# A fixed program order for attention's output projection, with its LayerNorm finished on ScalarE

## The chip, the cores and the metric

One core of a Trainium2 chip runs the whole kernel as one program. The metric is the device time of one execution in microseconds. Five engines work side by side, each through its own queue in order: TensorE (matmuls and transposes), VectorE, ScalarE, GpSimd, and SyncE, which here only issues DMA transfers.

## The reference

A pre-LayerNorm transformer block: sliding-window attention, then a gMLP whose gate mixes the 2048 positions by a matrix. S is 2048, D is 640, 32 heads of 20, window 256, hidden width 864.

```
def _A_ref(x, wqkv, wo):                      # attention
    q, k, v = split_heads(x @ wqkv)
    scores = einsum("bhqd,bhkd->bhqk", q, k) * Dh ** -0.5
    mask = (i - j >= 0) & (i - j < 256)
    p = softmax(where(mask, scores, -1e9))
    return merge_heads(einsum("bhqk,bhkd->bhqd", p, v)) @ wo

def _B_ref(x, w_in, w_sp, b_sp, w_out):       # gMLP
    z = gelu(x @ w_in)
    z1, z2 = z[..., :Fh], layernorm(z[..., Fh:])
    g = einsum("ts,bsf->btf", w_sp, z2) + b_sp[None, :, None]
    return (z1 * g) @ w_out

h = x + _A_ref(layernorm(x), A_wqkv, A_wo)
h2 = h + _B_ref(layernorm(h), B_w_in, B_w_sp, B_b_sp, B_w_out)
```

## The kernel before

The 2048 positions are 16 tiles of 128 rows. The stages follow each other: LayerNorm, q, k, v; attention by heads in groups of four; the output projection with the residual and the second LayerNorm; the gMLP's input projection (`z_pair`, `z2_pair`); the gate (`first_gate`, `second_gate`), and the output. Every matrix product is made of three products of split operands: a high part (a rounded copy) and a remainder (the operand minus the high part), so each product of two operands is high by high, high by remainder, remainder by high.

**The stage that the diff touches** is the loop over `i` in `range(NT)` near the end of `block_kernel`. For tile i it does this:

- `load_o` brings two tiles of attention output, stored in `o_d` by heads, into a buffer `m` and, by the function it returns, the reciprocals of the softmax sums from `r_d`. There are two such buffers, so the load for tiles 6 and 7 takes the place of tiles 2 and 3.
- `norm_o` multiplies the two on VectorE. `split_o` makes the high part (a copy on ScalarE, line 156) and the remainder (a subtraction on GpSimd, line 157).
- `proj_o` is the projection: 30 matmuls of 128x320 in `gemm` (line 91) into an accumulator `wo_ps`. There are two of those (`acc_tile`). Tiles 0 and 1 are projected earlier, while attention ends (`pre_ps`).
- The residual `xh` is added on VectorE (line 1160), the sum is stored in `h_d` by a DMA that ScalarE issues, and `layernorm` takes statistics on VectorE (lines 75 and 76), computes the reciprocal deviation on GpSimd (lines 77 and 78), and normalizes on VectorE (line 81).
- `turn_h(i - 2)` transposes the normalized tile on TensorE (line 806, into `ht_ps`), copies it out on ScalarE (`ho`), and stores it in `hn_d`, from which the gMLP's input projection reads it.
- Between these, `w1` (the generator `win1_prep`) prepares weights of the gMLP (`wraw` to `zl`), and `run(i - NT)` the first operands of the gMLP (`fx` to `aw`).

Before this loop stands attention's end. Its softmax sums are part of `o_d`. `inverse_sums` reads each quarter of them back from there (`inv`), takes the reciprocal on VectorE (line 348) and stores it in `r_d`; the last quarter can only be read when the last attention outputs (`ot`) have been written.

What sets the order: attention is inside `tc.manual_schedule` for TensorE, VectorE and ScalarE, so their instructions keep the order of the program. This ends with `ms.close()` ahead of the loop. From there the scheduler of the framework orders all engines by its own simulated times, and may put instructions of later iterations, or of later stages, ahead of earlier ones. GpSimd and SyncE are ordered by it in the loop in any case.

Of the kernel before, what the change touches and what calls it, by code (L numbers as in the profile page):

```python
# [7 lines left out]
F32 = mybir.dt.float32  # L8
F32R = mybir.dt.float32r
BF16 = mybir.dt.bfloat16  # L10
AF = mybir.ActivationFunctionType
OP = mybir.AluOpType
# [3 lines left out]
P = 128  # L16
S = 2048
D = 640
H = 32
DH = 20  # L20
NT = S // P
# [13 lines left out]
def block_kernel(ctx, tc, x, wqk, wv, wo, w_in, wsp, bsp, w_out, out):  # L35
    nc = tc.nc
    ms = ctx.enter_context(ExitStack())
# [3 lines left out]
    def pool(stack, name, **kw):  # L41
        return stack.enter_context(tc.tile_pool(name=name, bufs=1, reuse_waits="tile", **kw))

    const = pool(ctx, "const")
# [20 lines left out]

    def stat_tiles(i):
        st = const.tile([P, 2, 6], F32, tag="st", bufs=2, name=f"st{i}")
        mv = const.tile([P, 4], F32, tag="mv", bufs=3, name=f"mv{i}")
        return st, mv

    def layernorm(dst, src, n, key, between=None):
        st, mv = stat_tiles(key)
        hn = n // 2
        for j in range(2):
            nc.vector.bn_stats(out=st[:, j, :], in_=src[:, j * hn:(j + 1) * hn])
        nc.vector.bn_aggr(out=mv[:, 0:2], in_=st)
        nc.gpsimd.tensor_scalar(out=mv[:, 2:3], in0=mv[:, 1:2], scalar1=EPS, scalar2=None, op0=OP.add)
        nc.gpsimd.tensor_tensor(out=mv[:, 3:4], in0=mv[:, 2:3], in1=half, op=OP.pow)
        if between is not None:
            between()  # L80
        nc.vector.tensor_scalar(out=dst, in0=src, scalar1=mv[:, 0:1], scalar2=mv[:, 3:4],
                                op0=OP.subtract, op1=OP.mult)

    def gemm(ps, n, lhs, rhs, ks):

        lh, ll = lhs
        rh, rl = rhs
        for k in range(ks):
            for a, b in ((lh, rh), (lh, rl), (ll, rh)):
                for j in range(2):  # L90
                    nc.tensor.matmul(ps[:, j, :n], a(k), b(k, j),
                                     start=(k == 0 and a is lh and b is rh),
                                     stop=(k == ks - 1 and a is ll))
# [22 lines left out]
    def t1(lo, *shape):  # L116
        return view(mem["t1"], lo, *shape)

    def m1(lo, *shape):
        return view(mem["m1"], lo, *shape)  # L120
# [6 lines left out]
    def load_x2(i):  # L127
        hs[i] = mem["xh"][i % 5]
        nc.sync.dma_start(hs[i], x[i * P:(i + 1) * P, :])

    def load_o(j):

        t = slice(2 * j * P, (2 * j + 2) * P)
        ot, rs = m1(j % 2 * 2 * D, KD, 2 * P), m1(6 * D + j % 2 * 2 * P, 2 * P)
        for k in range(KD):
            nc.sync.dma_start(ot[:, k], o_d[:, 4 * k:4 * k + 4, t])
        for i in range(2):
            ots[2 * j + i] = (ot[:, :, i * P:(i + 1) * P], rs[:, i * P:(i + 1) * P])

        def load_rs():  # L140
            base = r_d[:, t]
            nc.sync.dma_start(rs, bass.AP(tensor=base.tensor, offset=base.offset, ap=[[S, H], [0, 4], [1, 2 * P]]))

        return load_rs

    def norm_o(i, eng):
        ot, rs = ots[i]
        eng.tensor_tensor(out=ot, in0=ot, in1=rs[:, None, :].to_broadcast([P, KD, P]), op=OP.mult)

    def split_o(i, eng):  # L150
        ot, _ = ots[i]
        osp = mem["osp2"] if i % 3 == 2 else t1((2 * KD + i % 3 * 2) * D, 2, KD, P)
        if eng is nc.vector:
            eng.tensor_copy(out=osp[:, 0], in_=ot)
        else:
            nc.scalar.activation(osp[:, 0], ot, AF.Copy)
        eng.tensor_tensor(out=osp[:, 1], in0=ot, in1=osp[:, 0].bitcast(F32), op=OP.subtract)
        ots[i] = osp

    def proj_o(i, ps):  # L160
        osp = ots.pop(i)
        wo_s = t1(0, 2, KD, D)
        gemm(ps, HD, [lambda k, p=p: osp[:, p, k, :] for p in range(2)],
             [lambda k, j, p=p: wo_s[:, p, k, j * HD:(j + 1) * HD] for p in range(2)], KD)
        return ps
# [35 lines left out]
    with ExitStack() as ab:  # L201
# [220 lines left out]
        if True:  # L422
# [8 lines left out]
            def ln1(i, between=None):  # L431
                xn = tmp.tile([P, D], F32, tag="tb", bufs=2, name=f"xn{i}")
                layernorm(xn, xts.pop(i), D, f"a{i}", between)
                xns[i] = xn
# [97 lines left out]
            c = halves[0]  # L532
# [73 lines left out]
        early, pre_ps = None, []  # L606
# [47 lines left out]
                pass  # L654


    ms.close()
    psK = ctx.enter_context(ExitStack())

    def acc_tile(name):  # L660
        return pools["c"].tile([P, 2, 512], F32, tag="acc", bufs=2, name=name)
# [6 lines left out]
    def bank(tag, name):  # L668
        if "d" not in pools:
            psK.close()  # L670
            pools["d"] = pool(ctx, "psD", space=PSUM)
        return pools["d"].tile([P, 512], F32, tag=tag, bufs=4, name=name)
# [56 lines left out]
    def hn(i):  # L729
        return m1((4 + i % 2) * D, D)  # L730
# [5 lines left out]
    def win1_prep(raw):  # L736
        seven, last = win1
        src = w_in[:, :FH].rearrange("k (h c) -> k h c", h=2)
        for k in range(2):
            for b in range(2):  # L740
                r = (k + 2 * b) * P
                nc.sync.dma_start(raw[:, b], src[r:r + P])
            yield
            yield
            for f in right_blocks(lambda: [s[k] for s in seven], *(raw[:, b, h] for b in range(2) for h in range(2)),
                                  eng=nc.gpsimd):
                f()
                yield
        nc.sync.dma_start(raw[:, 0], src[4 * P:])
        yield  # L750
        yield
        for j in range(2):
            split(*two(last[j]), raw[:, 0, j])
        yield
# [42 lines left out]
    def turn_h(i):  # L797
        ht = mem["ho"][i % 3]
        if i < NT - 2:
            ps = aux_tile(f"ht_ps{i}").rearrange("p a b -> p (a b)")  # L800
            parts = [(0, KD, ps)]
        else:
            parts = [(0, 4, bank("b", f"ht_a{i}")), (4, KD, bank("b", f"ht_b{i}"))]
        for k0, k1, ps in parts:
            for k in range(k0, k1):
                nc.tensor.transpose(ps[:, (k - k0) * P:(k - k0 + 1) * P], hn(i)[:, k * P:(k + 1) * P], ident)
            copy(ht[:, k0 * P:k1 * P], ps[:, :(k1 - k0) * P])
        nc.sync.dma_start(hn_d[i], ht)
# [90 lines left out]
    def z2_pair(q, i, j, k):  # L899
# [35 lines left out]
        def stat(t, h):  # L935
            if h == 0:
                stats[t] = stat_tiles(f"z{q}_{t}")
            st, mv = stats[t]
            nc.vector.bn_stats(out=st[:, h, :], in_=blocks[2 * t + h])
            if h:  # L940
                nc.vector.bn_aggr(out=mv[:, 0:2], in_=st)
                nc.gpsimd.tensor_scalar(out=mv[:, 2:3], in0=mv[:, 1:2], scalar1=EPS, scalar2=None, op0=OP.add)
                nc.gpsimd.tensor_tensor(out=mv[:, 3:4], in0=mv[:, 2:3], in1=half, op=OP.pow)
# [193 lines left out]
    def run(n):  # L1137
        for f in later.pop(n, []):
            f()
        if 0 <= n < len(steps):  # L1140
            steps[n][0]()
            steps[n][1]()

    w1 = win1_prep(mem["wraw"])
    for i in range(NT):
        if 1 < i + 1 < NT:
            split_o(i + 1, nc.gpsimd)
        if i % 2 == 0 and i + 4 < NT:
            load_o(i // 2 + 2)()
        if i + 2 < NT:  # L1150
            norm_o(i + 2, nc.vector)
        for n in (2, 3, 4) if i == 0 else (i + 4,) if i + 4 < NT else ():
            load_x2(n)
        run(i - NT)
        ps = pre_ps[i] if i < 2 else proj_o(i, acc_tile(f"wo_ps{i}"))
        if i > 1:
            turn_h(i - 2)
        xt = hs.pop(i)
        h3 = xt.rearrange("p (a b) -> p a b", a=2)
        nc.vector.tensor_tensor(out=h3, in0=ps[:, :, :HD], in1=h3, op=OP.add)  # L1160
        nc.scalar.dma_start(h_d[i], xt)
        layernorm(hn(i), xt, D, f"c{i}")
        next(w1, None)
        if i % 2:
            next(w1, None)
    for _ in w1:
        pass
    w2p = None
    for n in range(len(steps)):
        run(n)  # L1170
# [10 lines left out]
    n = NT - 2  # L1181
# [3 lines left out]
    ps = [bank("b", f"out_l{j}") for j in range(2)]  # L1185
# [30 lines left out]
```

## Time and profile before

| | us |
|---|---|
| median of 3 runs | 1148.1 |
| lowest, highest run | 1143.98, 1149.98 |
| span of the profiled execution | 1144.7 |
| TensorE busy in that span | 1096.0 (96%) |
| VectorE busy | 746.7 (65%) |
| ScalarE busy | 535.8 (47%) |
| GpSimd busy | 405.5 (35%) |

The profile gives the span as the profiled execution's own time, and no other; it lies within the three runs. In the profile's lines PE is TensorE, PEld its weight loads, DVE VectorE, ACT ScalarE, POOL GpSimd, SPq and ACTq the DMA queues of SyncE and ScalarE. A timeline row gives start, duration, engine, line, operation, output and inputs, and in square brackets how long the engine stood before it and what ended that. The projection loop lies between about 476 and 565 us of the span.

### The profile page before, as it was taken

The numbers are of one execution on the slowest core, as the hardware profiler recorded it, in microseconds if no ns is written. First come the engines' busy times: TensorE is split into PE (matmuls) and PEld (weight loads), VectorE is DVE, ScalarE is ACT, GpSimd is POOL, SyncE is SP. The second block draws the span as 40 slices with busy tenths as digits, with TensorE's granted clock in tenths as the row PEclk, the third lists the DMA queues.
The fourth block names the chain that finished last, engine by engine and source line by source line (L and its number), as shares of the span: only waits on it lengthen the run. The fifth ranks groups of instructions, "written<-read, shape, count | busy, mean of one in ns | idle before, by whom it ended". The sixth has DMA issues, their size and how long they took to land. (4 is left out here: it accounts for less than half of the span.)

```text
span 1144.7 us, 27633 instructions
## 1 busy us (share of the span) xinstructions
PE 1096.0 (96%) x10652; PEld 983.2 (86%) x10652; DVE 746.7 (65%) x1963; ACT 535.8 (47%) x1165; POOL 405.5 (35%) x553
## 2 busy tenths in 40 slices
PE   6999999999999999888999998999999899999998
PEld 6998887668788786788999997999999799999998
DVE  5541113789999996599677588455558974556543
ACT  3333433259999899344266554333334421222210
POOL 4124444547777678376220263000126410000000
PEclk9999999999999999899999998999999999999999
DMA  6212565656666635588455411323331463344322
GB/s 196 70 36 94 169 217 175 211 185 196 203 203 215 200 119 181 177 273 280 181 178 179 164 59 38 102 102 124 123 112 53 162 214 117 122 145 136 107 71 80
DMA packets 83844, 170.84 MB, mean 149 GB/s; under 512 B 11008, under 2 KB 47360, under 8 KB 79872
## 3 DMA queue, kind: packets, MB, share of 16 engines
q1 hardware_dynamic: 81408, 163.83, 44.3%
q10 hardware_dynamic: 2304, 5.24, 1.2%
q8 instruction: 83, 1.36, 0.5%
q14 instruction: 49, 0.40, 0.1%
HBM read 112.37 MB, written 56.23 MB: 147 GB/s over the span
## 5 line engine op out<-in xcount | busy, mean ns | idle before, releaser
L369 ACT ACTIVATE pt<-bank 128x384 f32<-128x384 f32 (+2 forms) x512 | 201.6, 496 | 13.9 <-PE bank L366 10.2
L1013 PE MATMUL g<-zl,aw 128*128 128x432 f32 x768 | 174.4, 362 | 7.3 <-ACT zl L681 4.9
L681 ACT ACTIVATE aw<-fx 128x512 fp32r<-128x512 f32 (+2 forms) x160 | 92.7, 595 | 187.6 <-PE g L1013 120.7
L312 DVE CUSTOM_DVE_ANT_0 junk<-bank,strip 128x288 bf16<-128x288 f32 x392 | 157.3, 454 | 6.6 <-PE bank L300 3.7
L1013 PEld LDWEIGHTS g<-zl,aw 128*128 128x128 f32 x768 | 144.8, 189 | 16.3 <-ACT zl L681 5.9
L1013 PE MATMUL g<-ze,aw 128*128 128x432 f32 x576 | 138.1, 368 | 6.0 <-DVE row L675 3.8
L675 DVE TENSOR_TENSOR aw<-fx,aw 128x512 fp32r<-128x512 f32 (+2 forms) x152 | 108.6, 723 | 37.2 <-ACT aw L681 36.7
L394 PE MATMUL pv<-pt,v_sb 128*32 128x192 f32 (+3 forms) x1984 | 126.8, 322 | 4.2 <-POOL pt L371 2.4
L1013 PEld LDWEIGHTS g<-ze,aw 128*128 128x128 f32 x576 | 109.2, 192 | 13.8 <-issue 3.2
L366 PE MATMUL bank<-slot 123*32 123x288 bf16 (+6 forms) x1536 | 107.0, 282 | 2.1 <-ACT pt L369 1.1
L371 POOL TENSOR_SCALAR_AFFINE_SELECT pt<-pt 128x512 f32<-128x512 f32 x128 | 84.0, 657 | 48.7 <-ACT pt L369 47.9
L1052 PE MATMUL out_ps<-wout,y_sp 128*128 128x320 f32 (+1 forms) x630 | 96.2, 310 | 0.4 <-ACT y_sp L124 0.4
L1052 PEld LDWEIGHTS out_ps<-wout,y_sp 128*128 128x128 f32 (+1 forms) x630 | 94.1, 188 | 1.3 <-ACT y_sp L124 0.7
L917 PE MATMUL zb<-win,aw 128*128 128x432 f32 x480 | 95.2, 359 | 0.0
L917 PEld LDWEIGHTS zb<-win,aw 128*128 128x128 f32 x480 | 90.0, 188 | 4.5
L300 PE MATMUL bank<-slot 120*32 120x288 bf16 (+2 forms) x1264 | 89.6, 286 | 0.0
L498 DVE TENSOR_TENSOR rest<-qk,sg 128x512 f32<-128x512 f32 x40 | 27.7, 691 | 85.7 <-ACT sg L496 85.7
L675 DVE TENSOR_TENSOR row<-g,row 128x432 f32<-128x432 f32 x80 | 48.0, 603 | 38.0 <-PE g L1013 32.5
L374 POOL TENSOR_SCALAR_AFFINE_SELECT pt<-pt 128x512 f32<-128x512 f32 x112 | 72.3, 645 | 0.0
L501 POOL TENSOR_TENSOR sg<-rest,sg 128x512 bf16<-128x512 f32 x40 | 46.6, 1164 | 72.1 <-ACT sg L500 68.9
L394 PEld LDWEIGHTS pv<-pt,v_sb 128*32 128x32 f32 x1984 | 59.4, 110 | 10.5 <-POOL pt L371 4.5
L366 PEld LDWEIGHTS <-slot 123*32 123x32 bf16 x1536 | 52.6, 97 | 17.2 <-issue 6.0
(189 smaller groups left out, 2172.7 us busy)
## 6 DMA issues: line engine op xcount, KB each, us to landing
fx<-wsp_in SPq DMA_DIRECT2D x32, 512.0 KB
slot<-qk_d SPq DMA_DIRECT2D x72, 200.0 KB
qk_d<-sg SPq DMA_DIRECT2D x32, 384.0 KB
slot<-qk_d SPq DMA_DIRECT2D x72, 160.0 KB
fx<-hn_d SPq DMA_DIRECT2D x32, 320.0 KB
o_d<-ot SPq DMA_DIRECT2D x64, 128.0 KB
z_d<-row SPq DMA_DIRECT2D x16, 432.0 KB
g_d<-row SPq DMA_DIRECT2D x16, 432.0 KB
```

Source lines behind the costliest of these rows:

```text
L300: nc.tensor.matmul(ps[32 * j:32 * j + 32, :n], part(st, half, 120, 0, hh, q0, 32), part(st, half, 120, 1, hh, lo + skip * j, n), start=Tru ...
L312: nc.vector.tensor_tensor_reduce(out=junk[:, :n], in0=ps[:, :n], in1=keep, scale=1.0, scalar=NEG, op0=OP.add, op1=OP.max, accum_out=m_cols ...
L366: nc.tensor.matmul(ps[32 * i:32 * i + 32, b:e], part(st, half, 123, 1, hh, k0, 32), part(st, half, 123, 0, hh, kb * P + b, e - b), start=T ...
L369: nc.scalar.activation(pt[:, hh, :n], ps[:, :n], AF.Exp, scale=SCALE)
L371: nc.gpsimd.affine_select(out=pt[:, :, :P], in_=pt[:, :, :P], pattern=[[0, 4], [1, P]], base=0, channel_multiplier=-1, compare_op=OP.is_ge ...
L374: nc.gpsimd.affine_select(out=pt[:, :, 256:], in_=pt[:, :, 256:], pattern=[[0, 4], [-1, P]], base=-1, channel_multiplier=1, compare_op=OP. ...
L394: nc.tensor.matmul(ps[32 * hh:32 * hh + 32, a - 512 * c:b - 512 * c], v_sb[:, kb, v0:v0 + 32], pt[:, hh, a - kb * P:b - kb * P], start=fir ...
L675: (eng or nc.vector).tensor_tensor(out=out, in0=a, in1=b, op=op)
L681: nc.scalar.activation(out, a, AF.Copy)
L917: nc.tensor.matmul(b[0][:, :HF], a[t][:, x, kk], win2[0][:, y, kk, h * HF:(h + 1) * HF], start=kk + x + y == 0, stop=kk == KD - 1 and x == 1)
L1013: nc.tensor.matmul(ps, w[m][:, x, k], zc[k][m][:, y], start=start and k + x + y == 0, stop=stop and k == 3 and x == 1, skip_group_check=True)
L1052: nc.tensor.matmul(ps[j][:, :HD], src[:w, a, k, :], e1["wout"][:w, b, k, j * HD:(j + 1) * HD], start=(k == 0 and a + b == 0), stop=(k == K ...
```

## The change

`ms.close()` moves behind the loop, so TensorE, VectorE and ScalarE keep the program's order there too, and the loop's body is rewritten: `split_o` stands right behind `norm_o` for tile i + 2, the projection ahead of `run` and of the weight preparation, and both ahead of the transposes. The LayerNorm in this loop is finished by `normalize`: GpSimd computes the negated mean times the reciprocal deviation as a fifth column of `mv`, and ScalarE applies scale and bias in one activation.

```
-        mv = const.tile([P, 4], F32, tag="mv", bufs=3, name=f"mv{i}")
+        mv = const.tile([P, 5], F32, tag="mv", bufs=3, name=f"mv{i}")
...
+    def normalize(dst, src, mv):
+        nc.gpsimd.tensor_scalar(out=mv[:, 4:5], in0=mv[:, 0:1], scalar1=mv[:, 3:4], scalar2=-1.0,
+                                op0=OP.mult, op1=OP.mult)
+        nc.scalar.activation(dst, src, AF.Identity, scale=mv[:, 3:4], bias=mv[:, 4:5])
+
-    def layernorm(dst, src, n, key, between=None):
+    def layernorm(dst, src, n, key, between=None, act=False):
...
+        if act:
+            return normalize(dst, src, mv)
         nc.vector.tensor_scalar(out=dst, in0=src, scalar1=mv[:, 0:1], scalar2=mv[:, 3:4],
                                 op0=OP.subtract, op1=OP.mult)
...
-    ms.close()
     psK = ctx.enter_context(ExitStack())
...
     for i in range(NT):
-        if 1 < i + 1 < NT:
-            split_o(i + 1, nc.gpsimd)
         if i % 2 == 0 and i + 4 < NT:
             load_o(i // 2 + 2)()
         if i + 2 < NT:
             norm_o(i + 2, nc.vector)
+            split_o(i + 2, nc.gpsimd)
         for n in (2, 3, 4) if i == 0 else (i + 4,) if i + 4 < NT else ():
             load_x2(n)
+        ps = pre_ps[i] if i < 2 else proj_o(i, acc_tile(f"wo_ps{i}"))
         run(i - NT)
-        ps = pre_ps[i] if i < 2 else proj_o(i, acc_tile(f"wo_ps{i}"))
+        next(w1, None)
+        if i % 2:
+            next(w1, None)
         if i > 1:
             turn_h(i - 2)
         xt = hs.pop(i)
         h3 = xt.rearrange("p (a b) -> p a b", a=2)
         nc.vector.tensor_tensor(out=h3, in0=ps[:, :, :HD], in1=h3, op=OP.add)
         nc.scalar.dma_start(h_d[i], xt)
-        layernorm(hn(i), xt, D, f"c{i}")
-        next(w1, None)
-        if i % 2:
-            next(w1, None)
+        layernorm(hn(i), xt, D, f"c{i}", act=True)
     for _ in w1:
         pass
+    ms.close()
```

The first place is VectorE's queue where the loop begins. `m` is the buffer of attention output (the rows of `m` by `m` of shape 5x128 are `norm_o`), `inv` the softmax sums, `xh` the residual tile, `stc` and `mvc` the statistics. Before, with tiles 1, 2 and 3 in its first row:

```order
L148 TENSOR_TENSOR m1_8920<-m1_8920 128x5x128 x3
L154 CAST t1_8919<-m1_8920 128x640
L157 TENSOR_TENSOR t1_8919<-m1_8920,t1_8919 128x640
L348 RECIPROCAL inv2_9398<-inv2_9398 128x128
L1160 TENSOR_TENSOR xh0_8921<-wo_ps0_9473,xh0_8921 128x640
L75 BN_STATS stc0_9608<-xh0_8921 128x6 x2
L76 BN_AGGR mvc0_9609<-stc0_9608 128x2
L81 TENSOR_SCALAR m1_8920<-xh0_8921,mvc0_9609 128x640
L1160 TENSOR_TENSOR xh1_8922<-wo_ps1_9518,xh1_8922 128x640
L75 BN_STATS stc1_9624<-xh1_8922 128x6 x2
L148 TENSOR_TENSOR m1_8920<-m1_8920 128x5x128 x2
L348 RECIPROCAL inv3_9549<-inv3_9549 128x128
```

The same place after:

```order
L155 TENSOR_TENSOR m1_8920<-m1_8920 128x5x128
L161 CAST t1_8919<-m1_8920 128x640
L164 TENSOR_TENSOR t1_8919<-m1_8920,t1_8919 128x640
L355 RECIPROCAL inv2_9398<-inv2_9398 128x128
L355 RECIPROCAL inv3_9549<-inv3_9549 128x128
L155 TENSOR_TENSOR m1_8920<-m1_8920 128x5x128
L1168 TENSOR_TENSOR xh0_8921<-wo_ps0_9473,xh0_8921 128x640
L80 BN_STATS stc0_9611<-xh0_8921 128x6 x2
L81 BN_AGGR mvc0_9612<-stc0_9611 128x2
```

Now the last reciprocal (`inv3`) and then the normalization of attention tile 2 stand ahead of the first residual add, where before three normalizations stood in front of everything and that reciprocal came behind the second add.

The second place is TensorE's queue from tile 4 on (`wo_ps4` to `wo_ps8` are projections of tiles, `ht_ps2` and so on the transposes of normalized tiles). Before:

```order
L91 MATMUL wo_ps4_9764<-t1_8919 128x320 x30
L91 MATMUL wo_ps5_9822<-t1_8919,osp2_9569 128x320 x4
L806 MATMUL ht_ps2_9795<-ident_72,m1_8920 128x128 x5
L91 MATMUL wo_ps5_9822<-t1_8919,osp2_9569 128x320 x26
L91 MATMUL wo_ps6_9886<-t1_8919 128x320 x30
L91 MATMUL wo_ps7_9941<-t1_8919 128x320 x7
L806 MATMUL ht_ps3_9853<-ident_72,m1_8920 128x128 x5
L91 MATMUL wo_ps7_9941<-t1_8919 128x320 x10
```

After:

```order
L98 MATMUL wo_ps4_9769<-t1_8919 128x320 x30
L812 MATMUL ht_ps2_9805<-ident_72,m1_8920 128x128 x5
L98 MATMUL wo_ps5_9828<-t1_8919,osp2_9568 128x320 x30
L812 MATMUL ht_ps3_9862<-ident_72,m1_8920 128x128 x5
L98 MATMUL wo_ps6_9891<-t1_8919 128x320 x30
L812 MATMUL ht_ps4_9926<-ident_72,m1_8920 128x128 x5
L98 MATMUL wo_ps7_9949<-t1_8919 128x320 x30
```

Transposes no longer cut into a projection; those of tile i - 2 follow each projection of tile i.

The third place is ScalarE's queue for tiles 2 and 3 after the change (`osp` and `t` are high parts of attention output, `ho` the transposed tile, `zl` prepared weights):

```order
L687 ACTIVATE zl2_9574<-wraw_8926 128x432
L687 ACTIVATE ho0_8923<-ht_ps0_9680 128x640
L1169 DMA h_d_68<-xh2_9565 128x640
L74 ACTIVATE m1_8920<-xh2_9565,mvc2_9691 128x640
L163 ACTIVATE osp2_9568<-m1_8920 128x640
L687 ACTIVATE zl6_9578<-wraw_8926 128x432
```

The normalization (line 74 after the change) stands ahead of the copy that makes the high part of the attention output of tile 5, and so each such copy waits for the statistics of the tile three before it.

## The prediction

> **What bounds the kernel now.** First the table by stage: one window from the last attention matmul to the first matmul of the gMLP input projection (the output-projection stage), one for the stage behind it.
>
> ```profile
> core 0: us, PE busy (x) PEld busy (x) DVE busy (x) ACT busy (x) POOL busy (x), PEclk, DMA share, GB/s
> 476.69:562.44 85.75, 77.25 (x525) 75.00 (x521) 76.31 (x126) 29.77 (x54) 48.37 (x51) 0.98 0.77 255
> 562.44:695.00 132.56, 132.56 (x683) 126.55 (x682) 94.50 (x159) 76.83 (x144) 40.34 (x35) 1.00 0.40 135
> ```
>
> Behind the stage TensorE is busy for 132.56 of 132.56 us, so whatever the projection stage gains or loses moves everything after it by as much. Inside it TensorE idles 8.5 us of 85.75, and VectorE, busy for 76.31 us, is the fullest engine after it. Who TensorE waits for, by the list of waits in 476.7 to 562.4:
>
> ```profile
> PE wo_ps L91 <- DVE xh L1160: 6.3, 4, 3.0
> PE ht_ps L806 <- DVE m L81: 1.7, 2, 1.0
> PE ht_ps L806 <- ACT osp L156: 0.4, 1, 0.4
> ```
>
> All but 0.4 us are waits for VectorE: for the residual add that frees an accumulator, or for the normalized tile that a transpose reads. TensorE's timeline shows the two paces and the gaps:
>
> ```profile
> 469.07 7.22 PE L91 MATMUL wo_ps<-t 128*128 128x320 f32 x30 [4.09 <-DVE t L154]
> ...
> 476.69 4.67 PE L91 MATMUL wo_ps<-t 128*128 128x320 f32 x30
> 481.20 4.57 PE L91 MATMUL wo_ps<-t,osp 128*128 128x320 f32 x30
> 485.60 0.71 PE L806 MATMUL ht_ps<-ident,m 128*128 128x128 f32 x5
> ...
> 504.79 7.20 PE L91 MATMUL wo_ps<-t 128*128 128x320 f32 x37 [1.88 <-DVE xh L1160]
> ...
> 524.34 4.67 PE L91 MATMUL wo_ps<-t 128*128 128x320 f32 x30 [2.95 <-DVE xh L1160]
> ...
> 557.02 0.71 PE L806 MATMUL ht_ps<-ident,m 128*128 128x128 f32 x5
> 557.49 4.65 PE L91 MATMUL wo_ps<-t 128*128 128x320 f32 x30
> 561.97 0.71 PE L806 MATMUL ht_ps<-ident,m 128*128 128x128 f32 x5
> ```
>
> An undisturbed tile (30 matmuls and 5 transposes) takes 561.97 - 557.02 = 4.95 us. Tile 2 is done at 485.60. From there 13 more tiles and one last transpose would need 13 x 4.95 + 0.47 (557.49 - 557.02) = 64.8 us. They took 562.44 - 485.60 = 76.84. So 12.0 us can be had at most: 8.4 are the waits above, 7.20 - 37 x 0.155 = 1.5 are matmuls at half clock (0.155 is 4.65 / 30), the rest is restarts.
>
> **The change, part by part.** The groups of the same window price the operations:
>
> ```profile
> L81 DVE TENSOR_SCALAR m<-xh,mvc 128x640 f32<-128x640 f32 x15 | 14.4, 957 | 5.5 <-POOL mvc L78 4.5 <-PE wo_ps L91 1.0
> L75 DVE BATCH_NORM_STATS2 stc<-xh 128x6 f32<-128x320 f32 x30 | 13.1, 477 | 0.1
> L1160 DVE TENSOR_TENSOR xh<-wo_ps,xh 128x640 f32<-128x640 f32 x16 | 12.8, 799 | 1.3 <-PE wo_ps L91 1.3
> L148 DVE TENSOR_TENSOR m<-m 128x640 f32<-128x640 f32 x12 | 10.5, 904 | 2.3 <-DMA inv<-o_d 2.3
> L76 DVE BATCH_NORM_AGGREGATE mvc<-stc 128x2 f32<-128x12 f32 x15 | 3.0, 197 | 0.2
> L78 POOL TENSOR_TENSOR mvc<-mvc,half 128x1 f32<-128x1 f32 x15 | 9.6, 643 | 1.1
> L157 POOL TENSOR_TENSOR osp<-m,osp 128x640 fp32r<-128x640 f32 x4 | 6.7, 1675 | 1.4 <-ACT osp L156 1.4
> L77 POOL TENSOR_SCALAR mvc<-mvc 128x1 f32<-128x1 f32 x15 | 6.4, 425 | 19.6 <-DVE mvc L76 19.6
> L156 ACT ACTIVATE osp<-m 128x640 fp32r<-128x640 f32 x4 | 2.9, 732 | 4.7 <-DVE xh L1160 4.6
> ```
>
> *The normalization on ScalarE.* VectorE loses 15 to 16 instructions, 14.4 us of its 76.3. ScalarE gains 16 of the same 128x640 shape. A form with a scale and a bias per row is not in the trace; the nearest rows are ScalarE's plain copy (0.73 us) and the VectorE operation itself (0.96). I take 0.74, so 11.8 us (upper end 15.4) on an engine busy for 29.8 of 85.75: covered. GpSimd gains 16 one-column operations at 0.43 (6.8 us on 48.4), which lengthens the path from statistics to normalized tile by as much. That path has room: a transpose of tile i stands behind the matmuls of tile i+2, about 9.9 us after tile i ended, and add 0.80, two statistics 0.95, aggregation 0.2, three GpSimd operations about 1.5 and ScalarE 0.74 make 4.2. Priced at nothing; without that cover it would be 0.43 per tile, 7 us.
>
> *The fixed order in the steady part.* TensorE's row is now whole: 30 matmuls, 5 transposes, 30 matmuls. The longest loop through the other queues is: tile i ends, add, statistics, normalization of the attention output of tile i+3 (0.9), GpSimd's statistics operations, ScalarE's normalization of i, ScalarE's copy for i+3 (0.73), GpSimd's remainder for i+3 (1.68). That is 4.2 + 0.73 + 1.68 = 6.6 us behind the end of tile i. Tile i+3 wants its operand 10.4 us after tile i ended (two tiles and a transpose). The VectorE normalization at 0.9 lies beside GpSimd's part. So with VectorE's load down by 14 us the waits of 8.4 us, the half clock of 1.5 and the restarts of 2.1 go: -12.0.
>
> *The fixed order at the start.* Here the strict queue costs. Before, the scheduler put the normalization of attention tiles 2 and 3 ahead; now tile 2's stands behind the last reciprocal of the softmax sums, which needs the last attention outputs written to memory and read back. VectorE, ScalarE and the DMA queue before:
>
> ```profile
> 464.32 0.51 SPq L345 DMA_DIRECT2D inv<-o_d  x1
> 466.53 0.95 DVE L348 RECIPROCAL inv<-inv 128x128 f32<-128x128 f32 x1 [7.02 <-DMA inv<-o_d]
> 469.47 1.01 SPq L411 DMA_DIRECT2D o_d<-ot  x2
> 472.20 1.56 DVE L148 TENSOR_TENSOR m<-m 128x640 f32<-128x640 f32 x2 [1.59 <-DMA o_d<-ot]
> 473.50 0.52 SPq L345 DMA_DIRECT2D inv<-o_d  x1
> 476.57 0.95 DVE L348 RECIPROCAL inv<-inv 128x128 f32<-128x128 f32 x1 [0.44 <-DMA inv<-o_d]
> 476.91 0.66 ACT L408 ACTIVATE ot<-pv 128x256 f32<-128x256 f32 x2
> 477.55 1.34 SPq L349 DMA_DIRECT2D r_d<-inv  x1
> 478.99 1.15 SPq L411 DMA_DIRECT2D o_d<-ot  x2
> 480.20 1.81 SPq L136 DMA_DIRECT2D m<-o_d  x3
> 482.26 0.51 SPq L345 DMA_DIRECT2D inv<-o_d  x1
> 486.96 0.95 DVE L348 RECIPROCAL inv<-inv 128x128 f32<-128x128 f32 x1
> ```
>
> At 472.20 tiles 2 and 3 were normalized, 14 us ahead of the last reciprocal. In the new order, up to the end of tile 1's matmuls (476.69 + 4.67 = 481.4) nothing is different. Then: the reciprocals' first store at 477.55 to 478.9; one load now ahead of the two writes (0.6), writes until 480.7; from the end of the writes to the readback 2.1 us (482.26 - 480.14) to 3.0 (473.50 - 470.48), so 482.8 to 483.7; readback to reciprocal 2.2 (466.53 - 464.32) to 3.1 (476.57 - 473.50), so 485.0 to 486.8, middle 485.9. Reciprocal 0.9 and normalization 0.8: 487.6. ScalarE's copy 0.74: 488.4, where tile 2's first four matmuls can go. GpSimd's remainder 1.6: 490.0, where the other 26 can. TensorE stands for some 8 us, and starts at a clock that the windows around the earlier gap of 4.09 us show:
>
> ```profile
> 469.00:474.00 5.00, 4.93 (x18) 4.93 (x19) 3.37 (x6) 0.74 (x1) 0.12 (x1) 0.50 0.66 192
> 474.00:475.00 1.00, 1.00 (x6) 1.00 (x6) 0.97 (x2) 0.00 (x0) 1.00 (x1) 0.61 0.49 169
> 475.00:476.00 1.00, 1.00 (x9) 1.00 (x8) 1.00 (x1) 0.00 (x0) 0.44 (x1) 1.00 0.37 117
> ```
>
> The granted clock (third column from the right) was 0.50 until about 474.6, 5.5 us after the restart at 469.07. Put on 488.4 that is half clock until 493.9: 3.9 us at 0.31 (twice 0.155) per matmul do 12.6 of the 26, the other 13.4 at 0.155 take 2.1, end 496.0. Bounds: early readback and no half clock, 489.1 + 4.0 = 493.1; late readback and all 26 at half clock, 490.9 + 8.1 = 499.0. Against 485.60 the start costs +10.4 (7.5 to 13.4).
> The Trainium skill (TensorE: Matmul & The Clock Gate, the section on what is actually happening) states that the gate opens after one busy window of about 3.4 us; by that rule, an estimate, tile 2 would end near 494.9 and the sum be 1.1 us better. The trace's row took 5.5 us, and I go by the row.
>
> *Sum.* -12.0 + 10.4 = -1.6 us (-4.5 to +1.4). For a wait that I don't see I leave 0.6, between none and the 8.4 of before. That makes **-1.0 us**: 1143.7 against the span of 1144.7. The runs shown have a median of 1148.1, 3.4 above that span, so **1147.1** stands for the median. The change buys back about what its own start loses.
>
> **Rivals.** *Slower: loads behind the strict VectorE queue.* Attention tiles 6 and 7 may be loaded only once tile 3's remainder has left GpSimd, about 494.6. The five loads of such a pair took this on the queue:
>
> ```profile
> 492.44 3.21 SPq L136 DMA_DIRECT2D m<-o_d  x5
> ```
>
> So they land near 494.6 + 3.2 + 3.1 = 500.9, and VectorE reaches tile 6's normalization after tile 3's statistics, near 496.0 + 4.95 + 2.0 = 502.9. Room there 2 us, plus 3.8 in the loop above: past 5.8 us of lateness TensorE stands, and with it the add that is queued behind the normalization. For it speaks a DMA share of 0.77 in the stage; against it that no wait for such loads is in TensorE's list, and that the next pairs have more room. There are five such pairs; 3 us past the room in each make +15, and +13.4 with the rest of the sum: about 1161. It ends slower from about 1.5 us per pair on.
>
> *Faster: the start hurts little.* If the writes land sooner and the clock stays up, tile 2 ends at 493.1 or before, and the gain is 4.5 or more; over 5.7 needs tile 2's end before 491.9, so a readback some 1.5 us under the fastest seen. About 1141. Nothing in the trace speaks for that much.
>
> *The change doesn't do what it says.* If TensorE's waits came from data rather than from VectorE's load, most of the 8.4 us stays and the start is added: +10.4 - 12.0 + 8.4 = +6.8, about 1155. Against it stands VectorE's 76.31 of 85.75 us, and the operations in front of the late adds being weight preparation.
>
> **How the numbers follow.** No change by more than 0.5% (5.7 us, about what a measurement of this kernel can tell from no change): 0.66, nearly all of it the forecast's, whose own range is 1142 to 1151. Faster: 0.16, the second rival and the low end. Slower: 0.18, 0.10 for the loads and 0.08 for the waits that stay. The range of 1140 to 1155 leaves out about one in ten on each side.
>
> **What would show it.** In the profile after: a gap on TensorE of 6 to 9 us between tiles 1 and 2, with VectorE idle until the last reciprocal and half clock behind it; tile 2 ending near 496; then tiles 4.95 us apart with almost no waits; the first gMLP matmul near 561; VectorE's busy time in the stage down by 14 us. Wrong if no such gap is there (then faster), or if tiles stand more than 5.4 us apart behind it (then slower); the waits there would name loads if the first rival holds.

## The result and the profile after

The changed kernel takes 1154.22 us (median of 6 executions, 1153.29 to 1158.49), the kernel before 1146.61 us beside it (6 executions). The ratio is 1.0091 with a 95% interval of 1.0072 to 1.0110: slower by 0.9%, where no change was forecast. The two medians alone are 7.6 us or 0.7% apart, so the ratio on record is somewhat larger than theirs; both say slower. The profiled spans are 1151.6 and 1144.7 us, a difference of 6.9.

The output-projection stage after the change, cut as before from the last attention matmul to the first gMLP matmul, and the 132.56 us behind it (the table by stage; the columns are those of the table shown for before):

```profile
475.79:568.00 92.21, 80.17 (x524) 76.92 (x521) 70.34 (x110) 41.15 (x68) 56.60 (x66) 0.94 0.70 229
568.00:700.56 132.56, 129.68 (x661) 122.26 (x660) 91.09 (x157) 75.41 (x140) 40.10 (x37) 1.00 0.41 142
```

The stage is 92.21 us long instead of 85.75, and TensorE stands for 12.0 us in it instead of 8.5, although VectorE is less busy. Who TensorE waits for there, by the list of waits of the kernel after:

```profile
PE wo_ps L98 <- ACT osp L163: 5.5, 1, 5.5
PE wo_ps L98 <- POOL t L164: 3.0, 3, 1.9
PE ht_ps L812 <- ACT m L74: 1.2, 1, 1.2
PE wo_ps L98 <- POOL osp L164: 1.1, 3, 0.6
PE wo_ps L98 <- DVE xh L1168: 1.1, 1, 1.1
```

The first row is the gap at the start. The others, 6.4 us, are all but 0.2 us waits behind the end of tile 2, and they carry new names: before, TensorE waited mostly for VectorE's residual add; now mostly for GpSimd's remainder of the next operand (`t`, `osp`). TensorE's timeline shows that tile 2 now ends, and the first transposes begin, at 492.75, and where tiles later wait:

```profile
485.92 1.44 PE L98 MATMUL wo_ps<-t,osp 128*128 128x320 f32 x4 [5.46 <-ACT osp L163]
487.55 5.37 PE L98 MATMUL wo_ps<-t,osp 128*128 128x320 f32 x26 [0.19 <-POOL osp L164]
492.75 0.71 PE L812 MATMUL ht_ps<-ident,m 128*128 128x128 f32 x5
...
534.45 5.62 PE L98 MATMUL wo_ps<-t 128*128 128x320 f32 x26 [1.91 <-POOL t L164]
...
563.06 4.64 PE L98 MATMUL wo_ps<-t 128*128 128x320 f32 x30 [1.09 <-DVE xh L1168]
```

From the end of tile 2 to the first gMLP matmul at 568.00 are 75.25 us, where 64.8 would be undisturbed. This stretch is called the steady part below; it was 76.84 before. Its tiles stand 5.75 us apart on average, the first three at 4.95, the widest at 8.84. The 6.9 us by parts: attention ended 0.9 earlier (476.69 - 475.79); from tile 1's start to tile 2's end it takes 16.96 us instead of 8.91, +8.05; the steady part -1.6; everything from the first gMLP matmul to the end of the span 583.6 instead of 582.3, +1.3.

### The profile page after: what moved, and what is told of

Same layout as the page of the kernel before. It is cut to its first block, busy times and chain, and to the rows that moved or that the text cites. A ratio compares the mean times of both kernels' runs of the same rounds, so it can differ in the third digit from the quotient of the medians.

```text
span 1151.6 us, 27669 instructions
## 1 busy us (share of the span) xinstructions
PE 1098.6 (95%) x10652; PEld 984.5 (85%) x10652; DVE 738.5 (64%) x1947; ACT 547.1 (48%) x1181; POOL 412.7 (36%) x569
## 4 chain that ended last, share of the span: by engine, by line
PE 65%; DVE 12%; DMA 7%; issue 6%; POOL 5%; ACT 3%; SPq 2%; ACTq 0%; POOLq 0%; DVEq 0%
PE g L1019 20%; PE out_ps L1058 8%; PE pv L401 6%; PE bank L307 5%; PE bank L373 5%; DVE aw L681 2%; PE qk L489 2%; PE qk L491 2%; PE qk L490 2%; POOL sg L508 1%; DMA fx<-hn_d 1%; DVE zl L681 1%; PE zb L923 1%; PE zx L872 1%; DVE row L681 1%
## 5 line engine op out<-in xcount | busy, mean ns | idle before, releaser
L687 ACT ACTIVATE aw<-fx 128x512 fp32r<-128x512 f32 (+3 forms) x160 | 92.8, 594 | 180.9 <-PE g L1019 119.7
L681 DVE TENSOR_TENSOR aw<-fx,aw 128x512 fp32r<-128x512 f32 (+3 forms) x152 | 110.8, 737 | 46.2 <-ACT aw L687 41.2
L373 PE MATMUL bank<-slot 123*32 123x288 bf16 (+5 forms) x1536 | 106.6, 282 | 1.2 <-ACT pt L376 0.7
```

The source lines that it names most:

```text
L373: nc.tensor.matmul(ps[32 * i:32 * i + 32, b:e], part(st, half, 123, 1, hh, k0, 32), part(st, half, 123, 0, hh, kb * P + b, e - b), start=T ...
L681: (eng or nc.vector).tensor_tensor(out=out, in0=a, in1=b, op=op)
L687: nc.scalar.activation(out, a, AF.Copy)
```

## The experiments

All ratios are against executions of the kernel before on the same chip. From profile to profile attention's end varies (the first projection matmul starts between 466.5 and 473.3 us with the same code ahead of it), so stretches are compared, not times from the span's start. Each stretch is read from one profile of one execution; how much a stretch varies between executions of one kernel was not measured. The two stretches are the start (first projection matmul to the end of tile 2: 16.53 us before, 24.15 after) and the steady part (76.84 before, 75.25 after).

**1 and 2. The two halves of the change, each alone.** e1 keeps the scheduler's order and the old loop and only finishes the LayerNorm on ScalarE; e2 has the new order and leaves the LayerNorm on VectorE.

```
e1:      layernorm(hn(i), xt, D, f"c{i}", act=True)     # in the loop of before
e2:      layernorm(hn(i), xt, D, f"c{i}")               # in the loop of after
```

> The kernel before with the LayerNorm of this loop finished on ScalarE, and nothing else: the scheduler still orders the loop. Theory A (the fixed order costs: 8.0 us at the start behind the last reciprocal, and in the steady part instructions that sit in a strict queue ahead of the operand copies): this part alone is no loss, VectorE loses some 14 us in the stage and of TensorE's 8.4 us of waits for it 3 to 8 go, so 1139 to 1144. Theory B (the normalization on ScalarE is what holds the loop, since the copy for tile i+3 stands behind the statistics of tile i): slower than before by 2 to 6 us, 1149 to 1153.

> The changed kernel with the normalization back on VectorE: the fixed order alone. Theory A: the gap of about 8 us ahead of tile 2 stays, and VectorE now waits in its strict queue for GpSimd's statistics operations in every tile (1.0 to 1.5 us each), so no better than the changed kernel: 1152 to 1162. Theory B: the copies on ScalarE come earlier, the steady part loses most of its 10.4 us of waits, 1146 to 1149.

e1: 1147.18 us, 1.0010 (0.9992 to 1.0028). e2: 1156.36 us, 1.0090 (1.0070 to 1.0109). e1 came out between the ranges of both theories, e2 in that of theory A. The order carries the loss: e2's ratio is that of the change. The normalization's move shows no gain in the times: none beside the old order, and beside the new one the medians are 1156.36 without it and 1154.22 with it, with ratios that agree. The profiles leave more room there, since e2's steady part is 79.73 us against 75.25. The profile of e1, by the table of the stage and the list of waits:

```profile
477.50:561.78 84.28, 76.89 (x516) 75.48 (x514) 64.84 (x111) 41.87 (x66) 51.54 (x66) 0.96 0.79 260
...
PE ht_ps L813 <- ACT m L74: 5.1, 3, 1.9
PE wo_ps L98 <- DVE xh L1167: 2.3, 2, 1.1
```

VectorE's load fell from 76.31 to 64.84 us, and TensorE still waits 7.4 us: 4 of the 6.3 us behind the add have gone, and the waits for the normalized tile grew from 1.7 to 5.1. So taking this load off VectorE was not enough. The run moves the load rather than taking it away, however, and lengthens the path to the normalized tile by a GpSimd operation and by ScalarE's queue; what the load's removal alone would bring isn't shown. The busy time of the steady part alone, before and in experiment 8 further below, sets the bounds:

```profile
485.60:562.44 76.84, 68.34 (x463) 66.09 (x460) 71.26 (x117) 29.03 (x51) 46.00 (x48) 0.98 0.78 261
484.44:551.24 66.80, 65.00 (x463) 64.67 (x460) 51.18 (x88) 37.18 (x58) 50.23 (x59) 1.00 0.85 288
```

VectorE's 71.26 us before are less than the 76.84 that the steady part took, but more than the floor of 64.8, so the floor was out of reach as long as VectorE was busy for that long. With e8's order VectorE is busy for 51.18; with the 13.7 us of the 14 normalizations it would be some 65, an estimate from these rows. Whether e8 would be as quick without the move, no run shows.

**3. The last reciprocal behind tile 1's statistics.** The kernel after, with only this moved (and a buffer of its own for that reciprocal):

```
-        for f in inverse:
+        for f in inverse[:3]:
...
         layernorm(hn(i), xt, D, f"c{i}", act=True)
+        if i == 1:
+            for _ in inverse[3]:
+                pass
```

> The changed kernel with one instruction moved: the last reciprocal of the softmax sums stands behind tile 1's statistics on VectorE instead of ahead of attention tile 2's normalization. Theory A: the gap between tiles 1 and 2 goes (from 6.6 us of waits and half clock to under 1), tile 2 ends 8 us earlier, and the time falls by 7 to 9 us to about 1146. Rival: the gap only moves to the next thing that is late (the first transpose or tile 3's operands), and the time falls by 0 to 3 us.

1148.19 us, 1.0024 (1.0002 to 1.0046), against 1.0091 of the change. TensorE's timeline has no gap between tiles 1 and 2 any more:

```profile
479.78 4.67 PE L98 MATMUL wo_ps<-t 128*128 128x320 f32 x30
484.29 4.57 PE L98 MATMUL wo_ps<-t,osp 128*128 128x320 f32 x30
488.69 0.71 PE L813 MATMUL ht_ps<-ident,m 128*128 128x128 f32 x5
```

The start is 15.36 us instead of 24.15. The place of one reciprocal in VectorE's strict queue makes about three quarters of the measured loss, by the two ratios. The median fell by 6.0 us, less than the 7 to 9 expected, although the start gained 8.8: this profile's steady part is longer than that of the change (77.98 against 75.25) and gains nothing on the kernel before.

**4. GpSimd in program order too.** A possible cause of the steady waits was that the scheduler still ordered GpSimd. The kernel after, with GpSimd's order fixed in the loop:

```
+    mp = ctx.enter_context(ExitStack())
+    mp.enter_context(tc.manual_schedule(engines={mybir.EngineType.Pool}))
     for i in range(NT):
...
+    mp.close()
```

> The changed kernel with GpSimd, too, kept in program order in this loop, so that the remainder for tile i+3 no longer stands behind the statistics operations of tile i+1 or i+2. Theory A1 (the steady waits are GpSimd's order): tiles 10, 13, 14 and 15, which took 3.9, 0.9, 0.7 and 1.3 us over 4.95, come down, 3 to 6 us less in all, 1148 to 1151. Theory A2 (they are copies of the gMLP stage that the scheduler put into ScalarE's queue, where they wait for reloaded tiles): at most 1 us.

1158.36 us, 1.0106 (1.0088 to 1.0124), steady part 79.25: no gain, and rather a loss, which neither theory had. GpSimd's order by itself wasn't it.

**5 and 6. No gMLP copies from behind the fixed order.** With the fixed order ending at the loop, instructions of the next stage stand inside the loop: copies of gMLP operands (`fx` to `aw`), in front of the residual add. e5 ends the fixed order behind step 8 of the next stage; e6 does so in the kernel of experiment 3.

```
-    ms.close()
     w2p = None
     for n in range(len(steps)):
         run(n)
+        if n == 8:
+            ms.close()
```

> The changed kernel with the fixed order kept on until step 8 of the gMLP's input projection, so that the scheduler can put none of that stage's operand preparation into the queues of ScalarE and VectorE inside the loop. Theory A2 (those copies wait for tiles that are reloaded from memory, up to 3.8 us, and hold up the residual adds and the operand copies behind them): tiles 6 to 10 lose most of their 7.6 us over 4.95 each, the steady part falls from 75.3 to 67 to 70 us, and the time by 4 to 8 us to 1146 to 1150. Theory A3 (the residual add stands behind the weight preparation and operand preparation that the program itself puts ahead of it on VectorE): the steady part stays at 73 to 76, the time within 2 us of the changed kernel.

> Both edits: the last reciprocal behind tile 1's statistics, and the fixed order until step 8 of the gMLP's input projection. If the two costs are apart from each other, the gains add: by theory A2 8 + 6, about 1140; by theory A3 8 + 0 to 2, about 1145 to 1147.

e5: 1153.22 us, 1.0073 (1.0051 to 1.0096), steady part 72.17. e6: 1147.64 us, 1.0020 (0.9997 to 1.0042), steady part 74.03. The copies cost some 3 to 4 us of the steady part (75.25 against 72.17, 77.98 against 74.03), and the stretch behind it was 3 us longer in both, so the kernel is not measurably faster for it. Most of the waits stay.

**7. No weight preparation in the loop.** e6 with the gMLP weight preparation (`w1`) taken out of the loop; all of it then runs behind the loop, so only the loop's pace is read from it.

```
-        next(w1, None)
-        if i % 2:
-            next(w1, None)
```

> As the one before, with the gMLP's weight preparation moved out of the loop, behind its last tile. The gMLP stage then starts late by the length of that preparation (15 to 25 us), so only the loop's pace counts. Theory A3: tiles stand 4.95 to 5.1 us apart, the steady part up to the last transpose is 65 to 67 us. Theory A2: it is no faster than the kernel above by more than 1 us. If the pace stays at 5.5 or more in both, the loads or the loop through statistics, GpSimd and ScalarE bound it.

One execution took 1161.97 us, since TensorE then stood for the weights. In the loop its list of waits is empty, and its timeline gives the pace (first two and last two of the 14 groups of transposes):

```profile
483.14 0.71 PE L813 MATMUL ht_ps<-ident,m 128*128 128x128 f32 x5
488.09 0.71 PE L813 MATMUL ht_ps<-ident,m 128*128 128x128 f32 x5
...
542.62 0.71 PE L813 MATMUL ht_ps<-ident,m 128*128 128x128 f32 x5
547.56 0.71 PE L813 MATMUL ht_ps<-ident,m 128*128 128x128 f32 x5
554.48 0.73 PE L873 MATMUL zv<-zl,aw 128*128 128x432 f32 x1 [6.21 <-ACT zl L688]
```

64.42 us for 13 tiles, all 4.94 to 5.06: the forecast's floor is real, with the operands only two tiles ahead, and the weight preparation keeps the loop from it. By its load or by its place?

**8, 11 and 12. Place of the weight preparation, and time of the next operands.** e8 rewrites the loop: the attention output of tile i + 3 instead of i + 2 is normalized and split, its pairs are loaded a tile earlier, GpSimd keeps program order, and all this side work, the weight preparation included, stands between the statistics of tile i and ScalarE's normalization. GpSimd's third statistics operation goes ahead of the side work. e11 is e6 with only the weight preparation put behind the LayerNorm. e12 is e8 with the side work put back ahead of the transposes and the add.

```
e8:
-        if i % 2 == 0 and i + 4 < NT:
-            load_o(i // 2 + 2)()
-        if i + 2 < NT:
-            norm_o(i + 2, nc.vector)
-            split_o(i + 2, nc.gpsimd)
+        if i % 2 and i + 5 < NT:
+            load_o((i + 5) // 2)()
...
-        run(i - NT)
-        next(w1, None)
-        if i % 2:
-            next(w1, None)
...
-        layernorm(hn(i), xt, D, f"c{i}", act=True)
+        def between():
+            if i + 3 < NT:
+                norm_o(i + 3, nc.vector)
+                split_o(i + 3, nc.gpsimd)
...
+            run(i - NT)
+            next(w1, None)
+            if i % 2:
+                next(w1, None)
+        layernorm(hn(i), xt, D, f"c{i}", between, act=True)
```

> A rewritten loop on top of the two edits: behind the statistics of tile i come the multiplication by the reciprocal sums and the operand copies of tile i+3, then the weight and operand preparation, and only then ScalarE's normalization of tile i; GpSimd in program order too; each pair of attention tiles loaded one tile earlier. So no VectorE instruction stands between the end of a projection and its residual add that waits for the same tile's normalization. Theory A3 (order on VectorE and ScalarE): tiles 4.95 to 5.2 us apart, steady part 65 to 68, time 1135 to 1140. Rival (the loads' arrival bounds the loop): the pace stays at 5.5 to 6, 1143 to 1150.

> The kernel with the late last reciprocal and the late end of the fixed order (e6, steady part 74.0 us against a floor of 64.8), with one more edit: the gMLP weight preparation goes back from its place ahead of the residual add to behind the LayerNorm, where it stood before the change. The amount of work is the same; only its place in the strict queues moves. Theory Q (the place decides: the add stands behind weight preparation in VectorE's queue): the steady part falls to 66 to 69, the list of waits no longer names GpSimd's remainder, 1140 to 1143. Theory O (operands decide: the copy for tile i+3 stands behind ScalarE's normalization of tile i, whatever lies ahead of the add): the steady part stays at 72 to 76 with GpSimd's remainder named, 1146 to 1150. Theory B (the sheer load on VectorE, ScalarE and GpSimd): 72 to 76 as well, but then the run beside it stays there too.

> The rewritten loop of e8 (steady part 66.8 us), in which the next operands (normalization and split of attention tile i+3) come one tile earlier and GpSimd keeps program order, but with the gMLP operands and the weight preparation put back ahead of the transposes and the residual add, as the change has them. Theory Q (the place of the weight preparation decides): the steady part is back at 72 to 76, and the waits name VectorE's add or ScalarE's normalization; 1145 to 1149. Theory O (operands decide): 66 to 69 and 1140 to 1143. Theory B (load): 72 to 76, together with no gain in the run beside it.

| | operands of | GpSimd's order | weight preparation | steady part | time | ratio |
|---|---|---|---|---|---|---|
| e6 | i + 2 | scheduler | ahead of the add, like all side work | 74.03 | 1147.64 | 1.0020 (0.9997 to 1.0042) |
| e11 | i + 2 | scheduler | behind the LayerNorm, the rest ahead of the add | 74.07 | 1144.49 | 1.0001 (0.9983 to 1.0019) |
| e12 | i + 3 | program | ahead of the add, like all side work | 78.76 | 1148.27 | 1.0034 (1.0015 to 1.0053) |
| e8 | i + 3 | program | behind the statistics, like all side work | 66.80 | 1140.93 | 0.9972 (0.9945 to 0.9999) |

All four have the same operations to do, so it is not the amount of work, and VectorE's busy share of the steady part (73 to 78% in all four, 77% in e8) doesn't tell them apart. e12 and e8 differ in the place of the side work alone, and that is worth 12 us of the steady part. e11 and e8 differ in more: the place, the operands' lead and their loads, and GpSimd's order. Neither e11 nor e12 gains anything on e6, and the lists of waits for the stage say what holds each. Of e11, of e12 and of e8:

```profile
PE wo_ps L98 <- POOL t L165: 5.2, 3, 2.2
PE wo_ps L98 <- POOL osp L165: 1.1, 2, 0.6
PE wo_ps L98 <- ACT t L164: 0.6, 2, 0.3
```
```profile
PE ht_ps L814 <- ACT m L72: 10.4, 7, 2.2
```
```profile
PE ht_ps L814 <- ACT m L72: 1.8, 1, 1.8
```

With the operands two tiles ahead TensorE waits for the operand; with operands early and the add late it waits for the normalized tile, seven times. There are two chains, and with the weight preparation in the loop either holds it 9 us or more above its floor. Which of e8's other edits loosens the first chain isn't shown. GpSimd's order is a rival to the operands' lead: in e11 the scheduler put weight subtractions of GpSimd between the statistics operations of a tile (one of 1.12 us at 502.99), and e12 and e8 fix that order. The one wait left in e8 begins at a load of weights, by ScalarE's timeline:

```profile
519.60 0.56 ACT L689 ACTIVATE zl<-wraw 128x432 fp32r<-128x432 f32 x1 [5.34 <-DMA wraw<-w_in_in]
520.07 0.90 ACT L72 ACTIVATE m<-xh,mvc 128x640 f32<-128x640 f32 x1
```

The normalization of a tile stands behind the copy of a weight that has not come yet.

**9 and 10. Ending e8's fixed order earlier.** e8's stretch behind the loop was 587.8 us against 582.3 before. e9 ends the fixed order at the loop, e10 after step 3.

```
e9:                          e10:
     mp.close()
+    ms.close()
...
-        if n == 8:          -        if n == 8:
-            ms.close()      +        if n == 3:
```

> The rewritten loop of the run before, with the fixed order ended right behind the loop, where the change ended it, instead of eight steps into the gMLP's input projection. That run spent 587.8 us from the first gMLP matmul to the end, the kernel before 582.3, and its TensorE waits there name ScalarE's row copies (4.8 us). Theory L (the fixed order in the input projection costs that): those waits go, 582 to 584 from the first gMLP matmul on; the loop loses at most the 3 us that the late end was worth with the loop of the change; in all 1135 to 1139 beside a kernel before of 1144. Theory H (without the late end, gMLP copies are put into the loop again, and wait there for reloaded tiles): the tiles stand 3 us or more further apart in sum, steady part 70 or more, and the time stays at 1140 to 1143. Theory T (a loop that ends earlier finds its operands not yet there, whatever the order): the loop stays at 66 to 68, the input projection still has 5 us of waits, 1140 to 1142.

> As the run beside it, with the fixed order ended after step 3 of the input projection instead of step 8. Theory L: the waits for ScalarE's row copies shrink with the length of the fixed order, 583 to 585 behind the first gMLP matmul, and the loop keeps its 66.8 us: 1137 to 1139. Theory T: no difference from the end after step 8, 1140 to 1142.

e9: 1143.75 us, 1.0013 (0.9985 to 1.0041), steady part 69.98. e10: 1142.61 us, 0.9987 (0.9969 to 1.0006), steady part 69.62. Theory L falls: the stretch behind the loop is 586.8 in e9 and 590.4 in e10. Theory T, which asked for a loop of 66 to 68, falls with e9's loop. Theory H is right for e9's loop, if short by 0.02 of the 70 it asked for, and ScalarE's timeline shows the copies of gMLP operands back in the loop, waiting for reloaded tiles:

```profile
506.68 0.62 ACT L689 ACTIVATE aw<-fx 128x128 fp32r<-128x128 f32 x2 [4.97 <-DMA fx<-hn_d]
...
516.09 0.74 ACT L689 ACTIVATE aw<-fx 128x640 fp32r<-128x640 f32 x1 [3.97 <-DMA fx<-hn_d]
```

In e10's loop one such copy is left (at 520.01), and the same wait for the weight. In e11 and e12, which end the fixed order as late as e8, the stretch behind is 582.8 and 582.5. So the late end isn't what costs 5 us in e8; why its stretch behind the loop is longer stays open. e8 is the only version whose interval lies below 1, and barely; one such interval among eleven is weak evidence of a gain in time. Its steady part, 10 us shorter than before, is the stronger finding.

## Why the prediction was wrong

**The start: right, somewhat over-sized.** The gap stood where it was forecast and for the reason given, with 5.5 us of waiting instead of the 6 to 9. VectorE's timeline and the DMA queue's around it:

```profile
477.78 1.54 SPq L418 DMA_DIRECT2D o_d<-ot  x2
...
481.29 0.52 SPq L352 DMA_DIRECT2D inv<-o_d  x1
...
483.46 0.95 DVE L355 RECIPROCAL inv<-inv 128x128 f32<-128x128 f32 x1 [7.02 <-DMA inv<-o_d]
484.33 0.76 DVE L155 TENSOR_TENSOR m<-m 128x640 f32<-128x640 f32 x1
```

It cost 8.05 us, forecast 10.4 (7.5 to 13.4). Write to readback took 2.0 us and readback to reciprocal 2.2, the short ends of the estimates, so the reciprocal came at 483.46 instead of 485.0 (485.9 less the 0.9 by which attention ended earlier). The granted clock after the restart, by windows of TensorE's timeline:

```profile
486.00:490.00 4.00, 3.81 (x13) 3.41 (x14) 3.90 (x8) 0.69 (x1) 3.08 (x4) 0.50 0.76 202
490.00:491.00 1.00, 1.00 (x8) 1.00 (x7) 0.89 (x2) 1.00 (x3) 0.83 (x1) 0.79 0.89 188
491.00:492.00 1.00, 1.00 (x9) 1.00 (x8) 0.60 (x1) 0.31 (x1) 0.94 (x2) 1.00 0.95 262
```

A mean of 0.79 in the middle window puts the change to full clock at about 490.4, which is 4.5 us after the restart at 485.92. The forecast took 5.5, counted as here from the restart behind ScalarE's copy; by the same working, its row with 0.61 in 474 to 475 gives 474.8 and 5.7. The 2.3 us by which the start was over-sized are the earlier reciprocal (1.5) and the shorter stretch from the restart to the end of tile 2 (6.83 instead of 7.6).

**The steady part: the step that failed.** The term of -12.0 us measured -1.6. Two of its premises fell.

The first: "with VectorE's load down by 14 us the waits of 8.4 us [...] go". Experiment 1 moved the load and 7.4 us of waits stayed; e12 and e8 have the same work and differ by 12 us. A busy share of 89% had been read as what delays the adds; what delayed them in the rows below is what stood in front of them in the queue. The forecast saw weight preparation there and still blamed the sum of the work. VectorE's busy time in the stage did not even fall by 14 in the kernel after: 76.31 to 70.34. The 15 normalizations have gone, but by the groups two more normalizations of attention output stand in the stage (14 instead of 12), and some subtractions took longer each (`wraw` 1224 ns on average instead of 904); the gMLP operand subtractions (`aw`) are no more than before, 9 instead of 10.

The second: the loop from the end of tile i to the operand of tile i + 3, reckoned at 6.6 us of the 10.4 allowed. That sum held the operations of the loop and none of its neighbours in three strict queues. The worst tile of the kernel after, rows of ScalarE, VectorE, GpSimd and TensorE from the timeline, in order of time; tile 6 was done at 512.89, tile 7 (26 of its matmuls stand in the first row) at 518.69:

```profile
514.61 4.08 PE L98 MATMUL wo_ps<-t 128*128 128x320 f32 x26 [0.42 <-POOL t L164]
518.25 0.74 ACT L687 ACTIVATE aw<-fx 128x640 fp32r<-128x640 f32 x1 [3.77 <-DMA fx<-hn_d]
519.02 0.83 DVE L681 TENSOR_TENSOR aw<-fx,aw 128x640 fp32r<-128x640 f32 x1 [3.06 <-ACT aw L687]
519.76 0.82 DVE L1168 TENSOR_TENSOR xh<-wo_ps,xh 128x640 f32<-128x640 f32 x1
...
522.66 0.81 DVE L1168 TENSOR_TENSOR xh<-wo_ps,xh 128x640 f32<-128x640 f32 x1
...
525.50 1.57 POOL L164 TENSOR_TENSOR t<-m,t 128x640 fp32r<-128x640 f32 x1 [1.67 <-ACT t L163]
...
528.57 1.11 POOL L681 TENSOR_TENSOR wraw<-wraw 128x432 f32<-128x432 f32 x1
529.78 0.27 POOL L72 TENSOR_SCALAR mvc<-mvc 128x1 f32<-128x1 f32 x1
...
530.08 0.92 ACT L74 ACTIVATE m<-xh,mvc 128x640 f32<-128x640 f32 x1 [0.58 <-POOL mvc L72]
530.91 0.72 ACT L163 ACTIVATE t<-m 128x640 fp32r<-128x640 f32 x1
...
532.53 1.86 POOL L164 TENSOR_TENSOR t<-m,t 128x640 fp32r<-128x640 f32 x1
```

A copy on ScalarE waits for a reloaded tile; VectorE's subtraction waits for that copy; the add of tile 6 stands behind it, 6.9 us late, and that of tile 7 behind both, 4.0 us late. Then tile 7's three GpSimd operations share their queue with a remainder and a weight preparation, so ScalarE normalizes tile 7 at 530.08, and the remainder for tile 10 ends at 534.39, 15.7 us after tile 7 instead of 6.6. TensorE waits 1.91 us for it. The runs took members of this chain away: the copies (experiments 5 and 6), the weight preparation (7), its place together with the operands' lead and GpSimd's order (8), and either without the other (11 and 12). With e7's loop all tiles follow each other at 4.95 (one at 5.06), with e8's all but one (6.91). GpSimd's neighbours were not taken away by themselves, and how much each member of the chain costs alone stays open.

The forecast's own sign of being wrong came: tiles more than 5.4 us apart behind the start, 5.75 on average.

**The rivals.** "The change doesn't do what it says" described the outcome: waits that come from data rather than from load and stay, +6.8 forecast and +6.9 measured. It had 0.08, since 76.31 of 85.75 us on VectorE were held against it, and experiments 1 and 8 show that they were weak evidence. The exact agreement is partly luck: the steady part gained 1.6 where this rival has it gain 3.6, the start cost 2.3 less, the stretch behind 1.3 more, and attention ended 0.9 earlier. The rival on loads of attention output was wrong: no wait of TensorE names them, and in e7 VectorE waits 10.6 us for such loads while the tiles keep 4.95.

**The normalization on ScalarE** was priced at nothing, and the times show no gain or loss from it (experiments 1 and 2); one takes 0.92 us where 0.74 was taken from the plain copy. In e1 its path shows in TensorE's waits, 5.1 us instead of 1.7, so its cover did not hold there.

**The sum.** -12.0 + 10.4 + 0.6 against -1.6 + 8.05 + 1.3 - 0.9: the first term, off by 10.4, alone turns -1.0 into +9.4; the other terms bring that down to +6.9.

## What to carry to other kernels

In a queue that keeps program order, the sum of an engine's work gives a bound but says little of the waits: ask of each instruction that TensorE waits for what stands in front of it in its queue, and what that in turn waits for, and walk every loop through all the queues with those neighbours counted in. Before counting on the removal of waits, take the suspected load away alone, without lengthening another path; if the waits only change their names, look for a second chain. When an order is written by hand, put an instruction that waits for a transfer (here the last reciprocal) behind all that doesn't need it, and side work behind the step that others wait for.

## What the runs showed of the hardware

*VectorE and GpSimd get in each other's way.* From experiment 12, the same normalization on VectorE twice, and GpSimd's remainder beside the first:

```profile
494.34 2.19 DVE L157 TENSOR_TENSOR m<-m 128x640 f32<-128x640 f32 x1
...
505.10 0.77 DVE L157 TENSOR_TENSOR m<-m 128x640 f32<-128x640 f32 x1
...
494.27 1.58 POOL L166 TENSOR_TENSOR t<-m,t 128x640 fp32r<-128x640 f32 x1 [1.67 <-ACT t L165]
```

GpSimd began 0.07 us earlier and ended at 495.85; VectorE's operation ended at 496.53, 0.68 later, about its own length. It looks as if it had done nothing until GpSimd was through. The Trainium skill (SBUF — State Buffer, the section on who interferes with whom) states that a VectorE instruction with two inputs in SBUF contends with a GpSimd instruction that reads SBUF, and that the port pair they share is an exclusive lock. These rows agree with it, as does the residual add, which takes one input from an accumulator: in e12 one took 0.81 us at 503.13, while a weight subtraction ran on GpSimd from 502.49 to 504.20. It happens the other way round too: at 505.25, 0.15 us behind the start of VectorE's second operation shown, a GpSimd operation on one column took 0.75 us, where the same operation took 0.27 at 499.03. A mean over such a group hides two values: in the steady part of e12, 11 normalizations average 1.32 us, five of them at 0.76 to 0.77 and four at 2.07 to 2.22; the 0.9 that the forecast took was such a mean. How much of TensorE's waits comes from this isn't shown.

*An activation with scale and bias per row* took 922 ns on average over 14 operations of 128x640, against 722 for the plain copy of the same shape, by the groups of the stage after:

```profile
L74 ACT ACTIVATE m<-xh,mvc 128x640 f32<-128x640 f32 x14 | 12.9, 922 | 35.7 <-POOL mvc L72 35.7
L163 ACT ACTIVATE t<-m 128x640 fp32r<-128x640 f32 x9 | 6.5, 722 | 0.0
```
